# A recurrent-memory attention layer on one core: attention output, output projection and value rows moved one stage later

## The chip, the core and the metric

The kernel runs on one core of a Trainium2 chip. The metric is device time in microseconds of one execution. The core has five engines with instruction streams of their own: TensorE (PE in the profile, with PEld for its weight loads), VectorE (DVE), ScalarE (ACT), GpSimd (POOL) and SyncE (SP). SP computes nothing here and issues DMA transfers; ACT computes and can issue transfers too.

## The reference

Four layers follow each other: A, B, A, B. Layer B is a linear attention and isn't touched. Layer A cuts 2048 tokens into 64 segments of 32. Each segment is attended together with 8 memory rows, and the output of those 8 rows is the memory of the next segment, so segments run strictly one after the other.

```python
for s in range(n_seg):                       # 64 segments
    xs = x[:, s * seg_len:(s + 1) * seg_len, :]
    h = jnp.concatenate([mem, xs], axis=1)   # 8 + 32 rows, 640 wide
    q = jnp.einsum('btd,dhe->bhte', h, Wq)   # 32 heads of 192
    k = jnp.einsum('btd,dhe->bhte', h, Wk)
    v = jnp.einsum('btd,dhe->bhte', h, Wv)
    scores = jnp.einsum('bhqe,bhke->bhqk', q, k) * scale
    scores = jnp.where(mask[None, None], scores, -1000000000.0)
    p = _softmax(scores, axis=-1)
    o = jnp.einsum('bhqk,bhke->bhqe', p, v)
    o = jnp.einsum('bhte,hed->btd', o, Wo)
    mem = o[:, :M, :]
    outs.append(o[:, M:, :])
```

## The kernel before

A layer A has three parts. `A_pre` computes, for all segments at once, keys, queries and values of those 8 rows of each segment that don't depend on the memory, and stores them in DRAM (`kqb_d`, `vb_d`). `A_chain` runs the recurrence. `A_post` makes the attention output of those 8 rows, from what the chain stored in `otb_d`.

`A_chain` is a loop over 64 segments (`s`), each of four rounds (`r`) of 8 heads. Its order is written out by hand (`tc.manual_schedule()`): every engine runs its instructions in the order of the source. A round of the kernel before does this:

- Q projection (`keys_or_queries`, `project`, L443): 20 matmuls in 5 blocks of 4 that run side by side in four column groups of the array.
- From round 1 on, `attend` of the round before (L495), then `extra_v` (L434), two small transfers that bring 8 stored value rows for this round into the tile `V`.
- `to_rows` for Q (L455, L460 to L463): ACT copies PSUM to SBUF, DVE transposes into `QT`. Then `store_o` (L508), which copies the attention output to `OT`.
- K projection, `to_rows` for K (L457, into `KT`), then `wo_round` of the round before (L513): 48 matmuls of `OT` with the resident output weights, accumulated in `W`.
- `scores` (L477 mask, L484 keys by queries), exponential into `E` (L548), `extra_kq` on POOL for the next round (L426 to L430).
- V projection. After three of its five blocks stands the matmul with a block of ones that sums `E` (L557). Then Ln and Exp of the sums on ACT (L563, L564), the multiplication of `E` on DVE (L566), and `v_rows` (L469 on DVE, L471 on ACT), which copies the 32 value rows of four head pairs from PSUM into `V`, DVE and ACT in turn.

After round 3 the segment ends serially: `attend`, `extra_v` for the next segment, `hx_transpose` (L414, new token rows), `store_o` on ACT and DVE (L506), `wo_round`, transpose of `W` (L581), memory rows into `hT` (L582), and only then the next Q projection. With odd segments, `ob` goes out by four transfers (L586).

Part of the projection weights is not kept in SBUF. A table `STREAM` says how many of the five blocks of each of the twelve matrices per segment are loaded anew: two for most, one for V of round 1, none for K of round 0. They land in a ring of three tiles (`wring`, `DEPTH = 3`, L308). `refill` issues the load for the use three places on, after the projection that reads the tile. In the kernel before all loads of the chain, large and small, are issued by SP in source order. Most tiles (`V`, `E`, `OT`, `QT`, `KT`, `hT`) are single-buffered.

Of the kernel before, what the change touches and what calls it, by code (L numbers as in the profile page):

```python
# [100 lines left out]
class Kernel:  # L101
# [180 lines left out]
    def layer_A(self, xn_dram, at_dram, li):  # L282
# [6 lines left out]
        self.vb_d = dram.tile([NSEG, NR, 2, 8, 768], BF16, name=f"vb{li}")  # L289
# [35 lines left out]

    def A_pre(self, xn_dram, li, load, pieces):
# [4 lines left out]
        with tc.tile_pool(name=f"A{li}_pre", bufs=1) as pp, \  # L331
# [15 lines left out]
            vt = pp.tile([P, 2, 768], BF16, name="vst")  # L347
            for r in range(NR):
# [19 lines left out]
                for tb in range(NT):  # L368
                    for g in range(4):
                        ps = ps_.tile([P, 512], F32, name="ps_pre", tag="bank")  # L370
                        for b in range(KC):
                            nc.tensor.matmul(ps[:, 0:384], lhsT=xBTf[:, b, P * tb:P * tb + P],
                                             rhs=wv[b][:, 384 * g:384 * g + 384], start=(b == 0), stop=(b == KC - 1))
                        ev.copy(out=vt[:, g // 2, 384 * (g % 2):384 * (g % 2) + 384], in_=ps[:, 0:384])
                    for t2 in range(TP):
                        nc.scalar.dma_start(out=self.vb_d[:, r, :, TP * tb + t2, :], in_=vt[NSEG * t2:NSEG * t2 + NSEG, :, :])

    def A_chain(self, xn_dram, at_dram, li, load, pieces, wo):
# [4 lines left out]
        with tc.tile_pool(name=f"A{li}_ch", bufs=1) as sp, \  # L383
# [5 lines left out]
            V = sp.tile([P, 768], BF16, name="Vp")  # L389
# [18 lines left out]
            def load_rows(s):  # L408
                for g in range(4):
                    nc.sync.dma_start(out=Hx[32 * g + 8:32 * g + 32, :, :], in_=xv[0:24, s:s + 2, 160 * g:160 * g + 160])  # L410

            def hx_transpose(s):
                hT = sp.tile([P, KC, 32], BF16, name="hT", tag="hT")
                nc.vector.transpose(out=hT[:, :, :], in_=Hx[:, s % 2, :].rearrange("p (j b) -> p b j", b=KC))  # L414
                if s % 2 == 1 and s + 1 < NSEG:
                    load_rows(s + 1)
                return hT

            def load_kqb(s):
                kqb = sp.tile([P, NR, 192], BF16, name="kqb", tag="kqb")  # L420
                nc.sync.dma_start(out=kqb[:], in_=self.kqb_d[s])
# [10 lines left out]
            def extra_v(s, r):  # L432
                for G in range(2):
                    nc.sync.dma_start(out=V[64 * G + 32:64 * G + 40, :], in_=self.vb_d[s, r, G])  # L434
# [18 lines left out]
            def to_rows(ps, m):  # L453
# [4 lines left out]
                else:  # L458
                    rv = raw[:, :].rearrange("p (g i j) -> p g i j", i=3, j=32)
                    nc.vector.transpose(out=qv[:, :, 0, 8:40], in_=rv[:, :, 0, :])  # L460
                    nc.vector.transpose(out=qv[:, :, 3, 8:40], in_=rv[:, :, 2, :])
# [3 lines left out]
            def v_rows(ps, g, eng):  # L465
                o = V[64 * (g // 2):64 * (g // 2) + 32, 384 * (g % 2):384 * (g % 2) + 384]
                i = ps[32 * g:32 * g + 32, 0:384]
# [21 lines left out]
            def attend(E):  # L489
                O = pop.tile([P, 2, 512], F32, name="ps_o", tag="o")  # L490
                for x in range(2):
                    for v0, mm, e, i, row in ((0, 128, 0, 0, 0), (256, 128, 1, 2, 0), (128, 64, 0, 1, 0), (192, 64, 1, 1, 64)):
                        for G in range(2):
                            o0 = 120 * x + 40 * i
                            nc.tensor.matmul(O[row:row + mm, G, o0:o0 + 40],  # L495
                                             lhsT=V[64 * G:64 * G + 40, 384 * x + v0:384 * x + v0 + mm],
                                             rhs=E[64 * G:64 * G + 40, 80 * x + 40 * e:80 * x + 40 * e + 40],
                                             start=(x == 0 and v0 == 0), stop=(x == 1 and v0 == 192),
                                             tile_position=(64 * G, row), skip_group_check=True)
# [10 lines left out]
            def wo_round(W, r, OT):  # L510
                for c in range(12):
# [4 lines left out]

            for g in range(4):
                nc.sync.dma_start(out=Hx[32 * g:32 * g + 8, 0, :], in_=self.A_mem0[:, 160 * g:160 * g + 160])
# [6 lines left out]
            hT = hx_transpose(0)  # L525
            for s in range(NSEG):
                if s % 2 == 0:
                    ob = sp.tile([P, 2, 160], BF16, name="ob", tag="ob")
                otb = sp.tile([P, NR, 12, 8], BF16, name="otb", tag="otb")
                W = pop.tile([P, 512], F32, name="ps_w", tag="w")  # L530
                E = None
                for r in range(NR):
                    pq = keys_or_queries(hT, "Q", r)
                    if E is not None:
                        O, OT = attend(E)
                        extra_v(s, r)
                    to_rows(pq, "Q")
                    if E is not None:
                        store_o(O, OT, 0, "s")
                        store_o(O, OT, 1, "s")  # L540
                        nc.gpsimd.tensor_copy(out=otb[:, r - 1, :, :], in_=OT[:, :, 0:8])  # L541
                    pk = keys_or_queries(hT, "K", r)
                    to_rows(pk, "K")
                    if E is not None:
                        wo_round(W, r - 1, OT)
                    S = scores()
                    E = sp.tile([P, 160], BF16, name="E", tag="E")
                    nc.scalar.activation(out=E[:], in_=S[:, 0:160], func=ACT.Exp, scale=scale)  # L548
                    if r + 1 < NR:
                        extra_kq(kqb, r + 1)  # L550
                    elif s + 1 < NSEG:
                        kqb = load_kqb(s + 1)
                        extra_kq(kqb, 0)
                    pv = pqp.tile([P, 512], F32, name="ps_qkv", tag="qkv")
                    w = weights("V", r)
                    project(hT, pv, w, "V", range(KC - 2))
                    nc.tensor.matmul(S[:, 256:416], lhsT=self.ones_blk[:, :], rhs=E[:, :], start=True, stop=True,  # L557
                                     skip_group_check=True)
                    project(hT, pv, w, "V", range(KC - 2, KC))
                    if STREAM["V", r]:  # L560
                        refill()
                    rc = sp.tile([P, 160], F32, name="rc", tag="rc")
# [256 lines left out]
```

The softmax here doesn't subtract the row's maximum and nothing guards it: scores larger than these inputs give would overflow.

## Time and profile before

| what | value |
|---|---|
| median of 3 runs | 5683.79 us (5674.05 to 5689.94) |
| profiled execution, own time | 5693.49 us |
| its span, first to last instruction | 5690.9 us |
| mean granted TensorE clock | 0.881 |
| TensorE matmul, busy | 73% |
| VectorE, busy | 41% |
| ScalarE, busy | 37% |
| HBM traffic over the span | 229 GB/s |

The page's slices show the two layers A as two long stretches of about 275 GB/s, and layers B between and behind them with little traffic. The busy shares are means over both kinds of layer, so a question about the chain is put to windows inside it. In the timeline a row gives start and length in us, engine, line, what is written from what is read, and in brackets how long the engine stood idle before it and what ended that. In the chain of waits each row is a piece of the path, followed back from the end. Matmul lengths overlap since they are pipelined: the issue time of a group is read from start to start.

### The profile page before, as it was taken

The numbers are of one execution on the slowest core, as the hardware profiler recorded it, in microseconds if no ns is written. First come the engines' busy times: TensorE is split into PE (matmuls) and PEld (weight loads), VectorE is DVE, ScalarE is ACT, GpSimd is POOL, SyncE is SP. The second block draws the span as 40 slices with busy tenths as digits, with TensorE's granted clock in tenths as the row PEclk, the third lists the DMA queues.
The fourth block names the chain that finished last, engine by engine and source line by source line (L and its number), as shares of the span: only waits on it lengthen the run. The fifth ranks groups of instructions, "written<-read, shape, count | busy, mean of one in ns | idle before, by whom it ended". The sixth has DMA issues, their size and how long they took to land.

```text
span 5690.9 us, 186473 instructions
## 1 busy us (share of the span) xinstructions
PE 4165.3 (73%) x79816; PEld 2489.4 (44%) x79816; DVE 2323.7 (41%) x6110; ACT 2122.3 (37%) x5373; POOL 631.5 (11%) x3095
## 2 busy tenths in 40 slices
PE   3877777777777777727858777777777777777568
PEld 2744444444444444413337444444444444444333
DVE  2234344434444444238432344444344434442483
ACT  1234444444444444213112344444444444443230
POOL 0011111111111111000000111111111111110000
PEclk9989888889998889859979898898899888999789
DMA  8777777777777878540077787777787877885301
GB/s 269 184 268 274 278 270 280 273 268 279 275 278 273 282 269 283 164 131 1 22 217 192 249 279 273 279 274 275 269 292 273 279 269 272 282 284 178 117 23 34
DMA packets 537065, 1312.99 MB, mean 231 GB/s; under 512 B 215376, under 2 KB 339248, under 8 KB 536240
## 3 DMA queue, kind: packets, MB, share of 16 engines
q1 hardware_dynamic: 361648, 1223.99, 61.7%
q10 hardware_dynamic: 174592, 77.09, 5.5%
q8 instruction: 629, 10.31, 0.7%
q14 instruction: 196, 1.61, 0.1%
HBM read 1213.43 MB, written 87.46 MB: 229 GB/s over the span
## 4 chain that ended last, share of the span: by engine, by line
PE 47%; DMA 23%; DVE 18%; ACT 7%; issue 3%; ACTq 1%; SPq 0%; DVEq 0%; POOL 0%; POOLq 0%
PE ps_qkv L443 20%; DMA wring<-wstK 9%; DVE Vp L469 7%; PE ps_o L495 6%; PE ps_w L513 5%; DMA wring<-wstQ 4%; DVE KT L457 3%; ACT raw L455 3%; PE ps_pre L358 3%; ACT Vp L471 3%; PE ps_s L484 2%; PE ps_num L627 2%; PE ps_bqk L627 2%; PE ps_kv L627 2%; DMA Vp<-vb 2%
## 5 line engine op out<-in xcount | busy, mean ns | idle before, releaser
L443 PEld LDWEIGHTS <-hT 128*32 128x32 bf16 x30720 | 739.3, 103 | 799.0 <-issue 410.0
L469 DVE CAST Vp<-ps_qkv 32x384 bf16<-32x384 f32 x1024 | 563.6, 550 | 1121.7 <-PE ps_qkv L443 960.1
L443 PE MATMUL ps_qkv<-wring,hT 128*32 128x384 bf16 x10752 | 749.2, 353 | 146.7 <-DMA wring<-wstQ 97.5
L495 PE MATMUL ps_o<-E,Vp 40*128 40x40 bf16 (+1 forms) x8192 | 507.7, 197 | 423.0 <-DVE Vp L469 253.2
L455 ACT ACTIVATE raw<-ps_qkv 128x384 bf16<-128x384 f32 x1024 | 501.9, 490 | 520.8 <-PE ps_qkv L443 498.9
L471 ACT ACTIVATE Vp<-ps_qkv 32x384 bf16<-32x384 f32 x1024 | 493.3, 482 | 519.4 <-DVE Vp L469 519.4
L513 PE MATMUL ps_w<-wo_res,OT 128*32 128x160 bf16 x24576 | 618.8, 259 | 72.8 <-ACT OT L508 71.8
L495 PEld LDWEIGHTS <-Vp 40*128 40x128 bf16 (+1 forms) x8192 | 319.3, 100 | 749.4 <-DVE Vp L469 315.6
L513 PEld LDWEIGHTS <-OT 128*32 128x32 bf16 x24576 | 539.0, 108 | 134.2 <-ACT OT L508 86.0
L443 PE MATMUL ps_qkv<-wQ,hT 128*32 128x384 bf16 x6144 | 407.1, 377 | 117.0 <-DVE hT L582 85.5
L460 DVE STREAM_TRANSPOSE QT<-raw 128x128 bf16<-128x128 bf16 x512 | 159.4, 311 | 726.2 <-ACT raw L455 726.2
L443 PE MATMUL ps_qkv<-wK,hT 128*32 128x384 bf16 x7168 | 455.4, 377 | 0.0
L443 PE MATMUL ps_qkv<-wV,hT 128*32 128x384 bf16 x6656 | 403.9, 340 | 2.7 <-issue 2.7
L457 DVE STREAM_TRANSPOSE KT<-raw 128x384 bf16<-128x384 bf16 x512 | 295.9, 578 | 250.1 <-ACT raw L455 248.2
L548 ACT ACTIVATE E<-ps_s 128x160 bf16<-128x160 f32 x512 | 155.2, 303 | 610.3 <-PE ps_s L484 610.3
L484 PE MATMUL ps_s<-QT,KT 128*40 128x40 bf16 (+1 forms) x6144 | 183.9, 190 | 239.4 <-DVE KT L457 239.1
L508 ACT ACTIVATE OT<-ps_o 128x240 bf16<-128x240 f32 x896 | 290.1, 368 | 101.5 <-PE ps_o L495 85.0
L426 POOL COPY QT<-kqb 128x32 bf16<-128x32 bf16 x512 | 106.7, 208 | 1975.3 <-PE ps_s L484 1032.3
L484 PEld LDWEIGHTS <-KT 128*40 128x40 bf16 x6144 | 140.8, 100 | 299.4 <-issue 298.4
L541 POOL COPY otb<-OT 128x96 bf16<-128x96 bf16 x384 | 100.7, 262 | 1405.6 <-ACT OT L508 1405.6
L563 ACT ACTIVATE rc<-ps_s 128x160 f32<-128x160 f32 x512 | 155.4, 304 | 263.4 <-PE ps_s L557 263.4
L358 PE MATMUL ps_pre<-xBT,wring 128*128 128x128 bf16 x1344 | 184.4, 221 | 4.4 <-DMA wring<-in_A_Wq_dram 3.2
(388 smaller groups left out, 4828.9 us busy)
## 6 DMA issues: line engine op xcount, KB each, us to landing
wring<-wstQ SPq DMA_DIRECT2D x516, 768.0 KB
wring<-wstV SPq DMA_DIRECT2D x387, 768.0 KB
wring<-wstK SPq DMA_DIRECT2D x387, 768.0 KB
wring<-wstV SPq DMA_DIRECT2D x129, 384.0 KB
kqb<-kqb SPq DMA_DIRECT2D x128, 192.0 KB
Vp<-vb SPq DMA_DIRECT2D x1024, 12.0 KB
wo_res<-in_A_Wo_dram SPq DMA_DIRECT2D x8, 1920.0 KB
kqb<-stk ACTq DMA_DIRECT2D x32, 384.0 KB
```

The source lines that it names most:

```text
L358: nc.tensor.matmul(ps[:, P * i:P * i + P], lhsT=w[b][:, P * c:P * c + P], rhs=xBT[:, b, :, 16 * tb:16 * tb + 16], start=(b == 0), stop=(b ...
L443: nc.tensor.matmul(ps[32 * g:32 * g + 32, 0:384], lhsT=hT[:, b, :], rhs=rhs, start=(b == 0), stop=(b == KC - 1), tile_position=(0, 32 * g) ...
L455: nc.scalar.activation(out=raw[:], in_=ps[:, 0:384], func=ACT.Copy)
L457: nc.vector.transpose(out=KT[:, :, 0:32], in_=raw[:, :].rearrange("p (c j) -> p c j", j=32))
L460: nc.vector.transpose(out=qv[:, :, 0, 8:40], in_=rv[:, :, 0, :])
L469: nc.vector.tensor_copy(out=o, in_=i)
L471: nc.scalar.activation(out=o, in_=i, func=ACT.Copy)
L484: nc.tensor.matmul(S[64 * G:64 * G + 40, c0:c0 + q1 - q0], lhsT=KT[:, 3 * g + i, :], rhs=QT[:, g, q0:q1], start=False, stop=False, tile_po ...
L495: nc.tensor.matmul(O[row:row + mm, G, o0:o0 + 40], lhsT=V[64 * G:64 * G + 40, 384 * x + v0:384 * x + v0 + mm], rhs=E[64 * G:64 * G + 40, 8 ...
L508: nc.scalar.activation(out=o, in_=i, func=ACT.Copy)
L513: nc.tensor.matmul(W[32 * g:32 * g + 32, 0:160], lhsT=OT[:, c, 8:40], rhs=wo[:, 12 * r + c, 160 * g:160 * g + 160], start=(r == 0 and c == 0),
L627: nc.tensor.matmul(ps[rows, n0:n0 + nn], lhsT=lhsT_fn(k), rhs=rhs_fn(k, n0, nn), **kw)
```

## The change

The rounds of `A_chain` are put in another order. In round r the order on TensorE is now: Q projection, K projection, attention of round r-1, V projection, scores, five of twelve steps of the output projection of round r-1, the sums of `E`, the other seven steps. The sums of round 0 stand after two blocks of round 1's Q projection. Normalisation (`normalise`) stands behind the output projection, and the value rows are copied around the exponential of the scores. The serial end of a segment keeps its steps, but `hx_transpose` moves ahead into round 3, with `hT` in two buffers.

`V` becomes 1024 columns wide: each head's 192 columns get 64 columns of zeros beside them (`two_heads`), and all attention matmuls have 128 output rows and one tile position per half. `vb_d` and `A_pre` follow this.

All small transfers of the chain (`load_rows`, `load_kqb`, `extra_v`, the stores of `otb` and of `ob`) move from SP's queue to ACT's; `kqb` of the next segment is loaded in round 2; the stores of `otb` and `ob` are issued in round 0 of the next segment. Two query transposes become one instruction, and the second half of `store_o` goes to DVE in all rounds.

```diff
-        self.vb_d = dram.tile([NSEG, NR, 2, 8, 768], BF16, name=f"vb{li}")
+        self.vb_d = dram.tile([NSEG, NR, 2, 8, 1024], BF16, name=f"vb{li}")
...
+    def two_heads(self, ap):
+        d = [list(x) for x in ap.ap]
+        return ap3(ap, [d[0], [320, 2], [1, 192]])
...
-            vt = pp.tile([P, 2, 768], BF16, name="vst")
+            vt = pp.tile([P, 4, 512], BF16, name="vst")
+            nc.vector.memset(vt[:], 0.0)
...
-            V = sp.tile([P, 768], BF16, name="Vp")
+            V = sp.tile([P, 1024], BF16, name="Vp")
...
-                    nc.sync.dma_start(out=Hx[32 * g + 8:32 * g + 32, :, :], in_=xv[0:24, s:s + 2, 160 * g:160 * g + 160])
+                    nc.scalar.dma_start(out=Hx[32 * g + 8:32 * g + 32, :, :], in_=xv[0:24, s:s + 2, 160 * g:160 * g + 160])
...
-                nc.sync.dma_start(out=kqb[:], in_=self.kqb_d[s])
+                nc.scalar.dma_start(out=kqb[:], in_=self.kqb_d[s])
...
-                    nc.sync.dma_start(out=V[64 * G + 32:64 * G + 40, :], in_=self.vb_d[s, r, G])
+                    nc.scalar.dma_start(out=V[64 * G + 32:64 * G + 40, :], in_=self.vb_d[s, r, G])
...
-                    nc.vector.transpose(out=qv[:, :, 0, 8:40], in_=rv[:, :, 0, :])
-                    nc.vector.transpose(out=qv[:, :, 3, 8:40], in_=rv[:, :, 2, :])
+                    nc.vector.transpose(out=qv[:, :, 0:4:3, 8:40], in_=rv[:, :, 0:3:2, :])
...
-                o = V[64 * (g // 2):64 * (g // 2) + 32, 384 * (g % 2):384 * (g % 2) + 384]
-                i = ps[32 * g:32 * g + 32, 0:384]
+                o = self.two_heads(V[64 * (g // 2):64 * (g // 2) + 32, 512 * (g % 2):512 * (g % 2) + 512])
+                i = ps[32 * g:32 * g + 32, 0:384].rearrange("p (e f) -> p e f", e=2)
...
-                    for v0, mm, e, i, row in ((0, 128, 0, 0, 0), (256, 128, 1, 2, 0), (128, 64, 0, 1, 0), (192, 64, 1, 1, 64)):
+                    for k, e, i in ((0, 0, 0), (3, 1, 2), (1, 0, 1), (2, 1, 1)):
                         for G in range(2):
                             o0 = 120 * x + 40 * i
-                            nc.tensor.matmul(O[row:row + mm, G, o0:o0 + 40],
-                                             lhsT=V[64 * G:64 * G + 40, 384 * x + v0:384 * x + v0 + mm],
+                            nc.tensor.matmul(O[:, G, o0:o0 + 40],
+                                             lhsT=V[64 * G:64 * G + 40, 512 * x + 128 * k:512 * x + 128 * k + 128],
                                              rhs=E[64 * G:64 * G + 40, 80 * x + 40 * e:80 * x + 40 * e + 40],
...
-                                             tile_position=(64 * G, row), skip_group_check=True)
+                                             tile_position=(64 * G, 0), skip_group_check=True)
```

The body of a round after the change, with `sums` and `normalise` as the new names of the matmul of L557 and of what was L562 to L566:

```python
pq = pqp.tile([P, 512], F32, name="ps_qkv", tag="qkv")
w = weights("Q", r)
project(hT, pq, w, "Q", range(2))
if r == 1:
    sums(S, E)
    normalise(S, E)
project(hT, pq, w, "Q", range(2, KC))
...
to_rows(pq, "Q")
pk = keys_or_queries(hT, "K", r)
to_rows(pk, "K")
if r == 0 and s > 0:
    nc.scalar.dma_start(out=self.otb_d[s - 1], in_=otb[:, :, :, :].rearrange("p r c t -> p (r c t)"))
    if s % 2 == 0:
        store_rows(s - 2, ob_old)
if r > 0:
    O, OT = attend(E)
    store_o(O, OT, 0, "s")
    extra_v(s, r)
    store_o(O, OT, 1, "v")
...
pv = pqp.tile([P, 512], F32, name="ps_qkv", tag="qkv")
project(hT, pv, weights("V", r), "V", range(KC))
if STREAM["V", r]:
    refill()
S = scores()
v_rows(pv, 0, "v")
v_rows(pv, 1, "s")
E = sp.tile([P, 160], BF16, name="E", tag="E")
nc.scalar.activation(out=E[:], in_=S[:, 0:160], func=ACT.Exp, scale=scale)
v_rows(pv, 2, "v")
v_rows(pv, 3, "s")
if r + 1 < NR:
    extra_kq(kqb, r + 1)
    if r + 2 == NR and s + 1 < NSEG:
        kqb = load_kqb(s + 1)
elif s + 1 < NSEG:
    extra_kq(kqb, 0)
    hT = hx_transpose(s + 1)
    if s % 2 == 0 and s + 2 < NSEG:
        load_rows(s + 2)
if r > 0:
    wo_round(W, r - 1, OT, range(5))
    sums(S, E)
    wo_round(W, r - 1, OT, range(5, 12))
    normalise(S, E)
```

## The prediction, made before the changed kernel ran

> **What bounds the kernel now.** I read the page's slices and DMA queues first, then the windows of one stretch, then the chain of waits over one segment boundary, then TensorE's timeline over one round. The memory update of L582 starts at 331.2 and 2311.0 us in the first A layer (63 times, 62 periods) and at 3195.3 and 5162.0 in the second: (1979.8 + 1966.7) / 124 = 31.83 us a segment, and 128 segments are 4074 of the 5690.9 us. Only they are changed in substance.
>
> Chain of waits, start, length, what:
> ```profile
> 1501.02 6.65 DMA wring<-wstV
> 1507.67 0.04 issue
> 1507.71 0.53 PE ps_qkv L443 x8
> 1508.24 0.02 issue
> 1508.27 0.56 DVE Vp L469
> 1508.82 0.02 issue
> 1508.85 0.49 ACT Vp L471
> ...
> 1511.50 1.36 PE ps_w L513 x48
> 1512.86 0.02 issue
> 1512.88 0.36 DVE wt L581
> 1513.24 0.02 issue
> 1513.26 0.24 DVE hT L582
> 1513.51 0.04 issue
> 1513.55 1.82 PE ps_qkv L443 x20
> ```
> Two things alternate: a weight load 6.65 us from issue to landing, and a serial tail. From the last V matmul (1508.24) to the next segment's first Q matmul (1513.55) is 5.31 us. The value rows are drained by DVE and ACT in turn, never together.
>
> TensorE timeline of a round without a load wait:
> ```profile
> 1517.70 0.35 PE L484 MATMUL ps_s<-QT,KT 128*40 128x40 bf16 x12 [1.21 <-DVE KT L457]
> ...
> 1521.02 0.87 PE L495 MATMUL ps_o<-E,Vp 40*128 40x40 bf16 x15 [0.68 <-DVE Vp L469]
> 1521.82 0.67 PE L443 MATMUL ps_qkv<-wK,hT 128*32 128x384 bf16 x12
> 1522.32 0.50 PE L443 MATMUL ps_qkv<-wring,hT 128*32 128x384 bf16 x8
> 1522.64 1.00 PE L513 MATMUL ps_w<-wo_res,OT 128*32 128x160 bf16 x48
> 1523.58 0.26 PE L477 MATMUL ps_s<-mask_st,ident 128*64 128x160 bf16 x2
> 1524.12 0.35 PE L484 MATMUL ps_s<-QT,KT 128*40 128x40 bf16 x12 [0.28 <-DVE KT L457]
> ```
> Scores to scores is 6.42 us. Starts give the issue times: a projection 0.82 (1521.82 to 1522.64), Wo 0.94, attention 0.80, scores 0.27. Twice a round TensorE stands: for value rows, and for transposed keys.
>
> Windows: two of rounds, one of the boundary; the last three columns are granted clock, DMA share, GB/s:
> ```profile
> 1519.00:1526.00 7.00, 5.93 (x162) 3.69 (x157) 3.17 (x9) 4.02 (x11) 1.38 (x7) 1.00 0.99 359
> 1528.00:1537.00 9.00, 7.61 (x194) 4.94 (x198) 3.97 (x13) 5.05 (x13) 1.50 (x7) 0.94 0.98 366
> 1513.00:1518.00 5.00, 3.24 (x58) 1.70 (x61) 2.04 (x7) 1.28 (x3) 0.60 (x3) 0.75 0.20 56
> ```
> In the rounds the DMA engines are full; at the boundary they are nearly empty, because the ring of three weight tiles is full, and no projection frees one. So a faster TensorE meets the loads.
>
> **What the Trainium skill says.** "TensorEngine Tiling (Array Packing)", Key Properties: a change of tiling mode drains TensorE. The trace agrees: 16 attention matmuls that alternate 64- and 128-column tiles take 0.80 us, 12 score matmuls of like size in one mode 0.27. "DMA: Bandwidth & Descriptors", Issuing engines are not separate DMA queues: another issuing engine saves only issue time, since the same 16 engines move the bytes. The trace has that time, 0.28 to 0.37 us of SP for each small transfer; no run shows yet what ACT pays for these. "TensorE: Matmul & The Clock Gate", HAM oscillation: idle gaps lower the array's clock. The trace agrees: the first 20 matmuls of a segment take 1.82 us against 0.96 later, and the boundary window has clock 0.75.
>
> **The change, part by part.** A round is now Q, K, attention of r-1, V, scores, 5/12 of Wo, softmax sums, 7/12 of Wo. From the diff and the durations above:
>
> *Waits that go.* Attention had waited for value rows and E (568.9 + 347.8 us over 512 rounds by the row of L495) and, for 68.4 us, for the vb transfer; now Q and K projections lie between (1.6 us). The normalisation (Ln 0.30, Exp 0.34, multiply 0.30) is hidden there too. Scores had waited 239.1 us for KT; raw copy 0.50 and transpose 0.58 now hide behind attention and V.
>
> *What is late next.* E. ACT has its first value copy ahead of E and waits for DVE's: after V's end 0.57 + 0.50 + 0.33 = 1.4 us to E, while TensorE has only scores 0.45 and five Wo steps 0.35. It stands about 0.6 us before the sums. Round: three projections 2.45 + attention 0.55 + 1.4 + sums and lag 0.4 + the rest of Wo 0.5 = 5.3 us, against 6.42.
>
> *Padded values.* Same matmul count; three mode changes go per attention. Bounds 0.36 (16 at the scores' rate) and 0.80; I take 0.55 with lag.
>
> *ACT transfers.* Fourteen issues per segment move to ACT (8 vb, 1 kqb, 1 otb, Hx and attn 2 each on average). At SP's 0.28 to 0.37 that is 4.6 us; ACT is busy 14.1 us of 31.8 (0.44), so no bound in sum. Upper price 0.62, as for vb<-vst on ACT. Queued behind: after the vb pair the value copy, already later because of DVE (no cost at 0.3); behind four attn stores E of round 0 (0.8 us every second segment, partly hidden by K1's load; I count nothing, 0.4 on average at most); behind four Hx loads Ln of round 3, on the tail: 4 x 0.36 = 1.4 us every second segment, 0.65 on average with overlap. The fourth Hx load also waits for the semaphore of the next Q0 load, which lands before by my times below. SP is freed: there four attn stores held the next weight load from 1514.09 to 1517.11.
>
> *Tail now.* V end to next Q: DVE 0.56, ACT 0.49, DVE 0.57, ACT 0.50 (2.16), Ln, Exp, multiply 1.0 with hand-overs (3.2), attention to 3.75, OT copy to 4.2, Wo 1.36 to 5.6, transpose and cast to 6.25. Against 5.31 it is 0.9 longer, because the normalisation now follows the value copies; with Hx 6.9.
>
> *Before the chain.* vb rows grow from 1536 to 2048 bytes. TensorE's waits on vb<-vst and what follows are some 65 us; a third would be 22, nothing the lower end. I take 6. Merged query transposes (0.31 to 0.58, I take 0.45) and the early hT transpose are off the path.
>
> **The loads.** A segment moves ten loads of 768 KB and one of half, 8.26 MB, and 0.54 MB of small things (0.57 after). At the 355 GB/s mean of full windows (359, 366, and 346 in another of 14 us) a load with its share of the small ones is 0.838 MB, 2.36 us. By the packet records of that boundary a load into an empty queue starts 1.0 us after issue, and TensorE goes on 1.1 to 2.0 us after its last packet; I take 1.4. A load issues when the projection three uses before it ends. From Q0's start (Q0 1.8 at low clock): projections end Q0 1.8, K0 2.7, V0 3.5, Q1 5.9. Then, landing and end: K1 6.6, 6.9; V1 7.75, 8.3; Q2 10.7, 11.4; K2 13.0, 13.35; V2 15.4, 15.75; Q3 17.75, 18.9; K3 20.1, 20.45; V3 22.45, 22.8. From K2 on the load, not TensorE, ends last at every step but Q3. With the tail the period is 29.7 us. It saves 2.1 us a segment: 128 x 2.1 = 270, less 6, from the profiled execution's own 5693.49 us (span 5690.9) gives about 5425. The shown median is 10 below it, so **5415 us**.
>
> The same reckoning for the kernel before gives about 30.5 where 31.83 was measured. It is short on scatter among loads, which is why the rivals below vary that term.
>
> **Rivals.** *The loads come slower still.* Packet records of loads that follow each other closely average 2.48 us; 7.5 loads lie between Q0 and V3, so 0.9 more: 30.7, a gain of 1.15 x 128 = 147, about 5540. For it: the shortfall just named. Against: small transfers no longer hold weight loads back on SP. Chance 0.25.
>
> *The clock stays up and loads run at the bare 2.21 us (0.786 MB at 355).* Q0 then takes 0.9 less, 7.5 x 0.15 = 1.1 less to V3, Wo in the tail 0.5 less: 27.2, 4.6 x 128 = 590, about 5095. For it: the tail has TensorE work in its first 2 us. Against: three idle stretches remain. Chance 0.20.
>
> *ACT becomes the bound, slower than before.* In-order ACT pays 0.62 per issue and waits for DMA semaphores: Hx +1.1 and the burst of otb and attn about +2.0 in every second segment, vb +0.26 in three rounds: 1.55 + 0.8 = 2.3 a segment, if the loads cover none. It decides from 2.1 us a segment; with the Hx loads' semaphore wait 0.4 more, 128 x 0.6 = 75: about 5750. For it: 0.62 stands in the trace for ACT. Against: that row is a 64-partition store, and a small store on ACT (attn<-obB) has 0.31. Chance 0.12.
>
> The order listing shows the moves as the diff has them, so that the change does nothing is no case.
>
> **How the numbers follow.** Forecast 0.43, own range 5330 to 5490 (period 29.0 to 30.3). Slower loads 0.25, better overlap 0.20, ACT 0.12. The whole range runs from 5100, which takes in most of the good case, to 5640, past the slow-load case at 2.6 us a load. No change that can be told means within 0.3%, 17 us: 0.03 lies there, from the slow-load case. Faster 0.85, slower 0.12.
>
> **What would show it.** Attention's idle time on value rows and E nearly gone; sums waiting for E at about 0.6 us a round; load waits of TensorE up from 146.7 us (the ps_qkv<-wring row) to some 500 (0.2 + 1.1 + 1.0 + 0.7 + 0.95 a segment above); the chain inside segments mostly weight loads; GB/s in the chain near 295 instead of 275; tails of 6.3 and 7.6 us in turn. Wrong would be: ACT stretches where its transfers sit between Exp and the value copies and TensorE waits for ACT; a load share under 0.85 with TensorE still waiting; or rounds above 6.4 us.

## The result, and the profile after

The changed kernel takes 5721.14 us (median of 4 runs, 5716.01 to 5736.02), the kernel before 5686.86 us beside it: a ratio of 1.0067, 95% interval 1.004 to 1.0094. It is a little slower, where 5415 us and a gain were forecast; the time lies above the whole range. The kernel before itself had medians from 5684 to 5724 us on different chips, so kernels are compared by their ratios to a kernel before that ran beside them, not by their times. The profiled execution took 5722.32 us, its span is 5720.5 us, and the mean granted clock fell from 0.881 to 0.870.

Since a segment keeps its steps, I cut the trace of each kernel at the same points and took means over the 124 boundaries: Q0 is the moment when the memory rows stand in `hT` (some 0.05 us before a segment's first Q matmul), V3 the start of the first value copy of round 3, and the tail runs from V3 to the next Q0. The period is the time from one Q0 to the next. These figures come from one profiled execution of each kernel; the four executions of one kernel lie up to 46 us apart (`norm_first`), which is 0.4 us a segment.

| us a segment | before | after | predicted after |
|---|---|---|---|
| Q0 to V3 | 26.43 | 24.22 | 22.8 |
| tail, V3 to next Q0 | 5.40 | 7.81 | 6.9 |
| of it, V3 to multiply done | 0.78 | 4.05 | 3.2, and 0.65 for Hx |
| to first and last attention matmul | 1.10, 2.43 | 4.32, 4.79 | 3.75 (last) |
| to start of Wo and to DVE's transpose behind it | 3.21, 4.83 | 5.50, 7.24 | 4.2, 5.6 |
| period | 31.83 | 32.03 | 29.7 |

So the rounds did gain 2.2 us and the tail gave back 2.4. In every second segment, nearly all of which load token rows (Hx), the tail is 8.23 us, in the others 7.39; 7.6 and 6.3 were predicted.

From the costliest groups of the page of the kernel after (line, engine, operation, tiles, count; busy and mean ns of one; idle time before it, and what ended most of that):

```profile
L452 PE MATMUL ps_qkv<-wring,hT 128*32 128x384 bf16 x10752 | 748.0, 353 | 367.3 <-DMA wring<-wstK 178.0
...
L503 PE MATMUL ps_o<-E,Vp 40*128 40x40 bf16 x8192 | 210.0, 181 | 301.6 <-DVE E L533 201.8
...
L526 PE MATMUL ps_s<-E,ones_blk 128*128 128x160 bf16 x512 | 120.7, 236 | 348.0 <-ACT E L582 348.0
...
L531 ACT ACTIVATE rc<-ps_s 128x160 f32<-128x160 f32 x512 | 155.3, 303 | 119.0 <-DMA Hx<-xn 101.8
```

The waits for streamed weights grew from 146.7 to 367.3 us, short of the 500 expected. The sums wait 348.0 us for `E`, 0.68 us a round, as predicted (0.6). The last row is ACT's: 101.8 us in which Ln stood behind the issues of the Hx loads.

The chain of waits of the kernel after, over one boundary and the round behind it (start, length, what), and the start of Ln in the tail that follows:

```profile
1508.77 0.27 ACTq L443
1509.04 0.06 ACT OT L516
1509.09 0.04 issue
1509.13 6.12 DMA Vp<-vb
1515.25 0.05 issue
1515.29 0.46 PE ps_o L503 x15
...
1516.26 1.82 PE ps_w L521 x47
...
1518.72 3.18 PE ps_qkv L452 x40
...
1522.83 0.38 ACTq L426
...
1545.97 0.38 ACTq L417
1546.36 0.04 issue
1546.40 0.38 ACTq L417
1546.78 0.04 issue
1546.82 0.38 ACTq L417
1547.20 0.05 issue
1547.25 0.31 ACT rc L531
```

Four things are to be seen. The attention of round 3 waits for the stored value rows (`Vp<-vb`, two transfers of 16 KB), which were under way for 6.12 us. `Wo` takes 1.82 us where the kernel before took 1.36 in the chain shown with the prediction (means: 1.74 and 1.62). The first 40 matmuls of the next segment take 3.18 us. And ACT, in order, issues `ob` stores (L426) and Hx loads (L417) on the path.

TensorE's timeline of the kernel after, over two rounds (start, length, line, tiles; in brackets the idle time before):

```profile
1530.19 0.23 PE L526 MATMUL ps_s<-E,ones_blk 128*128 128x160 bf16 x1 [0.83 <-ACT E L582]
...
1533.33 0.51 PE L452 MATMUL ps_qkv<-wring,hT 128*32 128x384 bf16 x8 [1.01 <-DMA wring<-wstK]
1533.77 0.37 PE L503 MATMUL ps_o<-E,Vp 40*128 40x40 bf16 x16
1534.07 0.67 PE L452 MATMUL ps_qkv<-wV,hT 128*32 128x384 bf16 x12
1535.60 0.51 PE L452 MATMUL ps_qkv<-wring,hT 128*32 128x384 bf16 x8 [0.87 <-DMA wring<-wstV]
...
1537.60 0.23 PE L526 MATMUL ps_s<-E,ones_blk 128*128 128x160 bf16 x1 [0.67 <-ACT E L582]
```

Inside the rounds the plan works: this attention starts with no wait at all (means of rounds 0 to 2: 0.17, 0.10 and 0.02 us, before 0.77, 0.64 and 0.25), and takes 0.30 us from start to start (1533.77 to 1534.07) instead of 0.80. What it waited for before has become two waits for weights, 1.01 and 0.87 us, in a round of 7.41 us.

### The profile page after: what moved, and what is told of

The parts are those of the page before. It is cut to its first block, busy times and chain, and to the rows that moved or that the text cites. A ratio compares the mean times of both kernels' runs of the same rounds, so it can differ in the third digit from the quotient of the medians.

```text
span 5720.5 us, 185022 instructions
## 1 busy us (share of the span) xinstructions
PE 3916.7 (68%) x79816; PEld 2351.5 (41%) x79816; DVE 2474.0 (43%) x5984; ACT 1969.5 (34%) x4989; POOL 630.8 (11%) x3095
## 4 chain that ended last, share of the span: by engine, by line
DMA 42%; PE 32%; DVE 11%; ACT 8%; ACTq 3%; issue 3%; SPq 1%; DVEq 0%; POOL 0%
DMA wring<-wstV 18%; PE ps_qkv L452 12%; DMA wring<-wstK 10%; DMA Vp<-vb 6%; PE ps_w L521 4%; ACT Vp L479 3%; PE ps_pre L364 3%; DVE Vp L477 3%; PE ps_num L653 2%; DMA vb<-vst 2%; PE ps_bqk L653 2%; PE ps_kv L653 2%; PE ps_o L503 2%; PE pp L630 2%; ACTq L417 1%
## 5 line engine op out<-in xcount | busy, mean ns | idle before, releaser
L452 PEld LDWEIGHTS <-hT 128*32 128x32 bf16 x30720 | 802.5, 104 | 1200.0 <-issue 823.6
L452 PE MATMUL ps_qkv<-wring,hT 128*32 128x384 bf16 x10752 | 748.0, 353 | 367.3 <-DMA wring<-wstK 178.0
L477 DVE CAST Vp<-ps_qkv 32x384 bf16<-32x384 f32 x1024 | 558.1, 545 | 496.5 <-ACT Vp L479 320.2
L521 PE MATMUL ps_w<-wo_res,OT 128*32 128x160 bf16 x24576 | 718.2, 267 | 67.8 <-ACT OT L516 66.8
L521 PEld LDWEIGHTS <-OT 128*32 128x32 bf16 x24576 | 509.4, 110 | 411.2 <-issue 310.0
L533 DVE TENSOR_TENSOR E<-E,rc 128x160 bf16<-128x160 bf16 x512 | 166.6, 325 | 693.6 <-ACT rc L532 693.6
L469 DVE STREAM_TRANSPOSE QT<-raw 128x256 bf16<-128x256 bf16 x512 | 228.0, 445 | 460.6 <-ACT raw L464 453.6
L503 PE MATMUL ps_o<-E,Vp 40*128 40x40 bf16 x8192 | 210.0, 181 | 301.6 <-DVE E L533 201.8
L526 PE MATMUL ps_s<-E,ones_blk 128*128 128x160 bf16 x512 | 120.7, 236 | 348.0 <-ACT E L582 348.0
L503 PEld LDWEIGHTS <-Vp 40*128 40x128 bf16 x8192 | 166.1, 95 | 453.7 <-issue 282.7
L514 DVE CAST OT<-ps_o 128x240 bf16<-128x240 f32 x512 | 208.9, 408 | 204.8 <-ACT OT L516 193.2
L516 ACT ACTIVATE OT<-ps_o 128x240 bf16<-128x240 f32 x512 | 188.3, 368 | 198.2 <-PE ps_o L503 192.0
L531 ACT ACTIVATE rc<-ps_s 128x160 f32<-128x160 f32 x512 | 155.3, 303 | 119.0 <-DMA Hx<-xn 101.8
```

The source lines that it names most:

```text
L452: nc.tensor.matmul(ps[32 * g:32 * g + 32, 0:384], lhsT=hT[:, b, :], rhs=rhs, start=(b == 0), stop=(b == KC - 1), tile_position=(0, 32 * g) ...
L469: nc.vector.transpose(out=qv[:, :, 0:4:3, 8:40], in_=rv[:, :, 0:3:2, :])
L477: nc.vector.tensor_copy(out=o, in_=i)
L503: nc.tensor.matmul(O[:, G, o0:o0 + 40], lhsT=V[64 * G:64 * G + 40, 512 * x + 128 * k:512 * x + 128 * k + 128], rhs=E[64 * G:64 * G + 40, 8 ...
L514: nc.vector.tensor_copy(out=o, in_=i)
L516: nc.scalar.activation(out=o, in_=i, func=ACT.Copy)
```

## The experiments

The theory after this reading: the loads take a part of what the rounds gain, and the tail takes the rest, through (a) Hx issues on ACT, (b) value rows that land last, (c) the normalisation behind the value copies, (d) a low clock. Rival: the loads alone set the period, so that whatever the tail gains is waited for again in the rounds. Ratios are to the kernel before, run beside each.

**1 and 2: which queue.** `hx_on_sp` is the kernel after with one issue back on SP, `small_on_sp` with all of the chain's small transfers there.

```diff
-                    nc.scalar.dma_start(out=Hx[32 * g + 8:32 * g + 32, :, :], in_=xv[0:24, s:s + 2, 160 * g:160 * g + 160])
+                    nc.sync.dma_start(out=Hx[32 * g + 8:32 * g + 32, :, :], in_=xv[0:24, s:s + 2, 160 * g:160 * g + 160])
```

> The changed kernel with its token-row loads (Hx) issued by SP instead of ACT. Theory 'the tail gives it back': these loads stand before Ln on ACT in every second segment's tail, where V to memory update is 8.23 us against 7.39 in the others, and Ln comes 1.66 us later. 62 such tails shorten by some 1.4 to 1.7 us: about 5620 us, ratio to before 0.985 to 0.99. Theory 'weight loads set the pace': what the tail saves comes back as load waits; 5700 to 5720, ratio 1.00 to 1.006.

> The changed kernel with all small transfers of the chain back on SP's queue; order of rounds and padding as changed. Theory 'the tail gives it back': as hx_on_sp, plus or minus little, 5600 to 5640. Theory 'the ACT queue's transfers land late' (the vb rows took 6 us from issue in one tail): still 0.3 to 0.5 us a segment better than hx_on_sp, 5560 to 5600. Theory 'SP holds the weight loads back again': slower than hx_on_sp by 0.5 to 1 us a segment, 5680 to 5740.

`hx_on_sp`: 5642.78 us, ratio 0.9875 (0.9823 to 0.9927). The multiplication ends 3.22 us after V3 in all segments, the tail is 7.40, the period 31.61. One edit turns a change that is 0.7% slower into one that is 1.2% faster. How much a segment gains is known only roughly: 0.42 us by the two traces, 0.9 us by the two ratios; the profiled execution of `hx_on_sp` was the slowest of its four, 5667.66 us. `small_on_sp`: 5745.26 us, 1.0044 (1.0026 to 1.0062), tail 8.28. That is near the 5680 to 5740 expected if SP held the weight loads back, but not for that reason: Q0 to V3 is 23.92 us, shorter than the 24.21 of `hx_on_sp`, and only the tail is longer. TensorE's waits for the value rows, first of `hx_on_sp`, then of `small_on_sp` (us in total, times, longest):

```profile
PE ps_o L503 <- DMA Vp<-vb: 188.1, 182, 3.0
```

```profile
PE ps_o L503 <- DMA Vp<-vb: 316.1, 125, 4.3
```

With Hx gone from the tail, the wait for these rows is twice as long as in the kernel after (86.1 us): they had been hidden under the Hx issues. On SP, where their issue also stands in order with the weight loads, they come later still. By the packet records (a packet is one piece that a DMA engine moves) the time from issue to the last packet is 4.03 us (median) in the kernel after and 4.25 in `small_on_sp`: ACT's queue is hardly a faster way in. What counts is what else is moving: in the kernel after the two transfers for round 0, issued in the tail when the DMA engines have little to do, are in after 1.33 and 1.37 us, the two for round 3 after 4.13 and 4.81 (medians).

**3 and 4: the loads.** Both kernels, with only the first of two streamed blocks loaded and used for both. The second block of those projections is left out of what is computed.

```diff
+                if short:
+                    nc.sync.dma_start(out=t[:, 0:1, :], in_=self.wst[m, r][:, 0:1, :])
...
-                return [res[m, r, b] for b in range(KC - ns)] + [t[:, i, :] for i in range(ns)]
+                return [res[m, r, b] for b in range(KC - ns)] + [t[:, 0 if short else i, :] for i in range(ns)]
```

> The kernel before, with only the first of the two streamed blocks of each weight loaded in the chain and used for both (the second block of the projection is left out of the loads, so the weights computed with differ); instructions on TensorE are the same. Theory 'weight loads set the pace': load waits go, period near 6.42 x 3 + 10.8 = 30.1 us, about 5460. Theory 'order alone': the same 5690.

> The changed kernel with the same halving of the streamed weights. Theory 'weight loads set the pace': its waits of TensorE for loads (367 us) go and rounds fall to the shortest seen, 5.2, 5.5, 5.5 and 10.7 us: period near 27, about 5100 to 5200, clearly under the halved kernel before (ratio of the two 0.93 to 0.95). Theory 'the tail and the ACT queue alone': it keeps its place, some 0.5% above the halved kernel before.

Before: 5546.35 us, 0.9715 (0.9674 to 0.9757), period 30.73. After: 5262.72 us, 0.9216 (0.9177 to 0.9256), period 28.45. Both are slower than expected (about 5460, and 5100 to 5200), but their ratio, 0.949, is as expected. The full loads cost the kernel before 1.10 us a segment and the kernel after 3.58, of which 3.16 lie between Q0 and V3; the other 0.42 are in the tail, where the small transfers land earlier too. With half the bytes the new order is worth 30.73 - 28.45 = 2.28 us; with all of them, -0.20. A round of the kernel before is 6.42 us between two exponentials, one of the kernel after 5.58 (medians), where 5.3 was predicted. TensorE of `half_loads_after` over one such round:

```profile
1506.17 0.35 PE L494 MATMUL ps_s<-QT,KT 128*40 128x40 bf16 x12 [0.29 <-DVE KT L468]
1506.45 0.53 PE L523 MATMUL ps_w<-wo_res,OT 128*32 128x160 bf16 x20
1507.81 0.23 PE L528 MATMUL ps_s<-E,ones_blk 128*128 128x160 bf16 x1 [0.83 <-ACT E L584]
...
1510.19 0.37 PE L505 MATMUL ps_o<-E,Vp 40*128 40x40 bf16 x16
...
1511.98 0.35 PE L494 MATMUL ps_s<-QT,KT 128*40 128x40 bf16 x12 [0.30 <-issue]
```

No wait for a load is left; `KT` (0.29) and `E` (0.83) hold the round. The prediction had the second (0.6), but not the first. The tail tells more: where no Hx load stands in it, it is 6.36 us, with attention right behind the multiplication (3.27 against 3.21). The prediction had 6.25 for just this tail. So the tail's own steps were sized well, and what came on top of them came from transfers.

**5: the padding alone**, on the kernel before.

```diff
-                                             lhsT=V[64 * G:64 * G + 40, 384 * x + v0:384 * x + v0 + mm],
+                                             lhsT=V[64 * G:64 * G + 40, 512 * x + 128 * k:512 * x + 128 * k + 128],
```

> The kernel before with the zero-padded value blocks alone (order of rounds and queues as before). Attention there is on the path in every round; padding takes three mode changes from it, 0.80 to some 0.45 us. Theory 'weight loads set the pace': a small part stays, 5640 to 5690, ratio 0.993 to 1.0. Theory 'TensorE's chain sets the pace': 512 x 0.35 = 180 us, about 5510, ratio 0.968.

5714.32 us, 0.9993 (0.9973 to 1.0012): no change, as expected if the loads set the pace. TensorE's timeline of `padding_alone`:

```profile
1520.84 0.27 PE L501 MATMUL ps_o<-E,Vp 40*128 40x40 bf16 x8 [0.68 <-DVE Vp L475]
1521.35 0.26 PE L501 MATMUL ps_o<-E,Vp 40*128 40x40 bf16 x7 [0.25 <-ACT Vp L477]
```

The matmuls are shorter, but in the old order they wait for value copies between them, so most of the time saved becomes idle time. The kernel before has that second wait too, hidden in the row of 15 matmuls in the prediction: by start times (medians) the tenth matmul comes 0.51 us after the second in both kernels, and the K projection behind attention 0.80 us after it before and 0.71 here. The change of tile size shows in the same start times: where the tile goes from 128 to 64 columns or back, the next matmul comes 0.11 to 0.14 us later in the kernel before, and 0.00 us later at the same places here.

**6: the normalisation.** `hx_on_sp` with Ln, Exp and multiplication of round 3 ahead of the last value copy and `hx_transpose` behind it.

```diff
-                    v_rows(pv, 3, "s")
+                    if r + 1 < NR:
+                        v_rows(pv, 3, "s")
...
                     normalise(S, E)
+                    if r + 1 == NR:
+                        v_rows(pv, 3, "s")
```

> hx_on_sp with Ln, Exp and the multiplication of round 3 ahead of the last value copy on ACT, and hx_transpose behind them. Theory 'the normalisation behind the value copies makes the tail long': multiply ends 0.9 us earlier than 3.22 after V, 128 x 0.8 = 100 us less than hx_on_sp, ratio 0.970. Theory 'the vb rows of round 3 land last': attention there already waits until 3.76 and its last matmul until 4.47 though E is ready at 3.22, so nearly nothing is gained, ratio 0.985 to 0.988.

5642.93 us, 0.9869 (0.9831 to 0.9906), the same as `hx_on_sp`. The multiplication ends 2.75 us after V3 instead of 3.22, and the last attention matmul starts at 4.41 instead of 4.47: the end that counted was another, the value rows.

**7 and 8: the value rows.** `vb_early` is `hx_on_sp` with the attention in round 3 ahead of the K projection, and with it the issue of that round's stored value rows. Since it also moves TensorE's work, `round3_rows_left_out` moves nothing: it is `hx_on_sp` without these two transfers in round 3.

```diff
+                        if r + 1 < NR:
+                            extra_v(s, r)
```

> hx_on_sp with attention ahead of the K projection in round 3, so that the vb rows of that round are asked for one projection and one load wait earlier. Theory 'the vb rows land last in the tail': last attention matmul 4.47 to 3.5 after V, 0.8 x 128 = 100 us less, ratio 0.970. Theory 'normalisation': no gain, 0.985 to 0.99.

> hx_on_sp, with the two transfers that bring the eight stored value rows of round 3 left out (V keeps those of round 2, so this part of the computation is not done); order and instruction counts are otherwise the same. Theory 'the tail's attention waits for these rows, which land last behind the weight loads': attention starts right after the multiplication (3.3 us after the first value copy of round 3 instead of 3.76 to 4.47) and the tail falls from 7.40 to 6.2 to 6.4 us; 126 segments x 1.1 = 139 us, some 5500 us, ratio 0.960 to 0.968, as in vb_early. Rival 'vb_early gained because the K projection behind the attention fills TensorE before the load of V': here nothing moves, the tail stays above 7.2 us and the ratio stays at hx_on_sp's 0.9875.

`vb_early`: 5519.31 us, 0.9637 (0.9605 to 0.9668), tail 6.26, period 30.49. `round3_rows_left_out`: 5534.2 us, 0.9715 (0.9686 to 0.9745), tail 6.35, period 30.54; its ratio lies a little over the 0.960 to 0.968 expected. In both the attention starts at 3.27 us, right behind the multiplication. The tail's chain of `round3_rows_left_out`:

```profile
1526.45 0.34 DVE E L533
1526.79 0.04 issue
1526.83 0.39 PE ps_o L503 x16
...
1527.72 1.07 PE ps_w L521 x48
```

Where 6.12 us of `Vp<-vb` stood, E leads into attention, and the multiplication ends at 3.22 us as before, so it is not ACT's time for two issues that was saved. So these rows cost 1.05 us a segment by the traces (7.40 - 6.35; by the ratios 0.7 in this kernel and 1.1 in `vb_early`), and starting their transfer one projection and its load wait earlier is enough to take the cost away. The rival falls for this term: the rounds, 24.2 us in all three kernels, took nothing back.

**9: the clock.** `hx_on_sp` with 28 matmuls whose result nobody reads, 20 ahead of the attention of round 3, 4 ahead of Wo and 4 behind it.

```diff
+            def keep_busy(S, n):
+                for _ in range(n):
+                    nc.tensor.matmul(S[:, 416:512], lhsT=self.ones_blk[:, :], rhs=self.mk[:, 0:96], start=True, stop=True,
+                                     skip_group_check=True)
```

> hx_on_sp with 28 matmuls of 96 columns, whose result nobody reads, in the tail's idle stretches of TensorE (20 before attention, 4 behind it, 4 behind Wo). Theory 'low clock in the tail and in Q0': Wo of the tail goes from 1.65 to some 0.95 us and Q0 with K0 from 3.2 to some 1.8; at least the tail's 0.7 us a segment shows, 90 us, up to 180 with Q0 and K0: ratio 0.956 to 0.972. Theory 'it costs or does nothing': 0.985 to 1.0.

5538.72 us, 0.9677 (0.965 to 0.9705), period 30.67. Windows of 4 us on either side of a boundary, first of `hx_on_sp`, then of `array_kept_busy` (window, length, busy time of PE, PEld, DVE, ACT, POOL with counts, then granted clock, DMA share, GB/s):

```profile
1506.25:1510.25 4.00, 2.33 (x64) 1.82 (x64) 0.94 (x3) 0.55 (x2) 0.26 (x1) 0.65 0.50 200
1510.25:1514.25 4.00, 3.94 (x52) 2.05 (x56) 0.94 (x4) 1.10 (x3) 0.00 (x0) 0.50 0.22 71
```

```profile
1515.46:1519.46 4.00, 2.96 (x89) 2.23 (x89) 1.08 (x4) 0.55 (x2) 0.26 (x1) 1.00 0.58 222
1519.46:1523.46 4.00, 3.46 (x82) 2.00 (x82) 1.95 (x6) 1.10 (x3) 0.29 (x2) 1.00 0.42 138
```

In the second row of each, the new segment gets through 52 and 82 matmuls in the same 4 us, at clock 0.50 and 1.00. The tail falls to 7.09 us and Q0 to V3 to 23.58: 0.94 us a segment for work that does nothing. Q0 and K0 together fall from 2.89 to 1.82 us, as expected; Wo of the tail falls to 1.23 us, not to the 0.95 expected.

**10: all of it.** `hx_on_sp` with the edits of `norm_first`, `vb_early` and 14 + 4 + 4 unread matmuls.

> hx_on_sp with norm_first, vb_early and 14 + 4 + 4 unread matmuls that keep TensorE busy in the tail. If the tail's terms are in series (theory), they add once the value rows land in time: multiplication at 2.75 us instead of 3.2, attention right behind it, Wo and Q0 at the higher clock: tail 5.2 to 5.5 us, Q0 to first value copy of round 3 about 23.6, period 28.7 to 29.2 us: 5290 to 5370 us, ratio 0.925 to 0.94. Rival 'the loads take back what the tail gains' (the ring is full at the boundary, so an earlier Q0 only waits longer for the same loads): period not under 30.2 us, 5480 to 5520 us, ratio 0.96 or more.

5410.47 us, 0.9508 (0.9475 to 0.9541), period 29.51, tail 5.90: faster than both kernels. It misses the 0.925 to 0.94 and the tail of 5.2 to 5.5 us expected. The chain of its tail shows what I had left out, the unread matmuls themselves (L537), which stand between Wo and attention:

```profile
1509.51 0.60 PE ps_w L521 x28
1510.11 0.70 PE ps_s L537 x14
1510.81 0.32 PE ps_o L503 x16
```

So attention starts at 3.05 us where the multiplication was done at 2.73; with these 0.32 us taken off, the tail would still be 5.58 us, and the rest of the miss was not traced. With 29.51 the rival's 30.2 is refuted: what the tail gains stays gained.

**11 and 12: the stores of `otb` and `ob`**, from `all_together`: moved on ACT behind the exponential and value copies of round 0, or to SP behind V0's load.

```diff
-                    if r == 0 and s > 0:
-                        nc.scalar.dma_start(out=self.otb_d[s - 1], in_=otb[:, :, :, :].rearrange("p r c t -> p (r c t)"))
...
                     v_rows(pv, 3, "s")
+                    if r == 0 and s > 0:
+                        nc.scalar.dma_start(out=self.otb_d[s - 1], in_=otb[:, :, :, :].rearrange("p r c t -> p (r c t)"))
```

> all_together with the stores of otb and ob moved on ACT's queue from ahead of the attention of round 0 to behind the exponential and value copies of that round. Theory 'the burst of stores holds E of round 0 back, with the rounds and all their loads behind it': in segments with the four ob stores the stretch from Q0 to the first value copy of round 3 was about 0.35 to 0.7 us longer; it becomes equal in both kinds, the mean falls from 23.62 to about 23.4 us or less, 126 x 0.2 to 0.35 = 25 to 45 us, ratio 0.943 to 0.947. Rival 'the load of K1 and V1 hides it': ratio stays at 0.951, the second load issue of a segment (V0) comes earlier, the later ones don't.

> all_together with the stores of otb and ob taken off ACT: SP issues them behind the load that V of round 0 frees. Theory 'five stores in a row occupy ACT for 2.1 us, and whatever ACT does next in round 0 or 1 waits': with ACT free, segments with the four ob stores reach the first value copy of round 3 as early as the others (23.3 to 23.45 instead of 23.79 us), mean 23.35 to 23.45 instead of 23.62, a gain of 126 x 0.2 = 25 us: ratio 0.944 to 0.948. Rival 'on SP the 2.1 us hold back the next weight load (that of Q in round 1) just as long': that load is issued when Q1 ends, about 2.8 us after V0's; if the stores are not done by then, the later loads of these segments come up to 0.5 us later and the ratio is 0.951 or more.

`stores_behind_E`: 5518.58 us, 0.9651 (0.9626 to 0.9676), where 0.943 to 0.947 was expected: worse than `all_together`. Timeline of one segment with the five stores:

```profile
1520.22 0.35 ACTq L592 DMA_DIRECT2D otb<-otb  x1
...
1520.67 1.64 ACTq L426 DMA_DIRECT2D attn<-ob  x4
...
1522.36 0.30 ACT L531 ACTIVATE rc<-ps_s 128x160 f32<-128x160 f32 x1 [1.71 <-DMA otb<-otb]
...
1523.44 0.37 PE L503 MATMUL ps_o<-E,Vp 40*128 40x40 bf16 x16 [1.87 <-DVE E L533]
```

The burst holds ACT from 1520.22 to 1522.31, and Ln stands behind it: TensorE waits 1.87 us. In these segments Q0 to V3 is 25.84 us, in the others 23.31. So the burst did hold `E` of round 0 back (in segments with the stores it comes 0.60 us later than in the others in `all_together`, 0.21 here), but its new place is worse than its old one. `stores_on_sp`: 5464.36 us, 0.9571 (0.9543 to 0.96), where 0.944 to 0.948 was expected. It is also worse than `all_together`, though only by 0.6%, and the two intervals all but touch. `E` of round 0 now starts 4.51 and 4.49 us after Q0, in segments without and with the stores, so ACT is freed as expected. But SP issues the load behind K1 at 8.13 us instead of 6.57 in the segments with stores; the trace names the `otb` store as what SP waited for (104.1 us in 52 cases). V3 is also 0.37 us later than in `all_together` in segments without stores; that was not traced to a cause.

## Why the prediction was wrong

The period was to be 29.7 us and was 32.03; 126 x 2.33 = 294 us, and 5415 + 294 = 5709 is close to the 5721 measured, so these segments account for the miss. It has two parts, 0.91 in the tail and 1.42 ahead of V3.

**The tail.** The step that failed is "Waits that go": the prediction took the 68.4 us that attention had waited for vb as a wait that goes, and never asked when the rows of the last round would land in the new order. They cost 1.05 us a segment (shown by experiments 7 and 8). The prediction had quoted that the same 16 engines move the bytes, and applied it to the price of issuing and not to the time of landing. The Hx issues were costed at 1.4 us every second segment, 0.65 on average; ACT's Ln comes 1.66 us later in these segments (3.85 against 2.19), and with the rows late anyway they cost 0.41 (7.81 - 7.40). The rest of the tail, 6.35 us with both gone, is near the 6.25 predicted. So the 0.91 is 1.05 for the rows, 0.24 less for Hx and 0.10 for the rest. Wo was taken from one row at 1.36, where its mean had been 1.62; it took 1.74 in the kernel after and takes 1.49 to 1.59 where the rows are not awaited.

**Ahead of V3.** By the issue times of the loads, which follow the end of a projection, in us after Q0:

| | V0 | Q1 | V1 | Q2 | V2 | Q3 | V3 |
|---|---|---|---|---|---|---|---|
| predicted | 3.5 | 5.9 | 8.3 | 11.4 | 15.75 | 18.9 | 22.8 |
| kernel after | 3.97 | 6.80 | 9.17 | 12.93 | 17.07 | 20.42 | 24.19 |
| array_kept_busy | 2.94 | 5.89 | 8.34 | 12.09 | 16.53 | 20.04 | 23.51 |

From Q2 to V3 the kernel after needs 11.26 us where 11.4 was predicted: the pace of the loads was right, and the rival of slower loads is not what happened. What failed is the start: 0.90 us by Q1, and 0.66 more from V1 to Q2 (3.76 instead of 3.1). The loads did not do this: with half their bytes Q1 and Q2 end at nearly the same times, 6.93 and 12.94 us. Three terms were mis-sized.

- The clock. A low clock was counted for Q0 alone, but K0 and V0 have it too: they take 2.12 us from the end of Q0 (the load issue at 1.85) where 1.7 was taken, and 1.71 with the clock kept up. "TensorE: Matmul & The Clock Gate", HAM oscillation, in the Trainium skill, names idle gaps as the cause of a lower clock, and the runs agree; the prediction had put a higher clock into a rival only.
- The stores ahead of `E` of round 0, "I count nothing". They make Q1 0.70 us later in every second segment (7.15 against 6.45), of which 0.51 is left at V3: 0.25 on average. In `small_on_sp`, where SP issues them, Q1 ends equally early in both kinds of segment (within 0.05 us).
- `E` of round 1, from V1 to Q2. It was to be done 1.4 us after the end of the V projection, with DVE's first value copy starting at once. That copy starts 0.60 us late (mean) and `E` is done at 1.98 us. DVE, in order, has other work first, as the timeline shows: the last V matmuls, then `KT`, then the second half of the copy to `OT`, which the change moves to DVE (L514), then the value copy (L477), ACT's copy behind it, and `E`.

```profile
1527.79 0.34 PE L452 MATMUL ps_qkv<-wring,hT 128*32 128x384 bf16 x4
1527.82 0.58 DVE L466 STREAM_TRANSPOSE KT<-raw 128x384 bf16<-128x384 bf16 x1
...
1528.43 0.41 DVE L514 CAST OT<-ps_o 128x240 bf16<-128x240 f32 x1
...
1528.76 0.54 DVE L477 CAST Vp<-ps_qkv 32x384 bf16<-32x384 f32 x1
...
1529.33 0.48 ACT L479 ACTIVATE Vp<-ps_qkv 32x384 bf16<-32x384 f32 x1 [1.73 <-DVE Vp L477]
...
1529.83 0.30 ACT L582 ACTIVATE E<-ps_s 128x160 bf16<-128x160 f32 x1
```

In rounds 2 and 3, where TensorE waits for loads, the same copy starts 0.05 and 0.08 us after V's end. With half the loads it is late in all three rounds (0.61, 0.42 and 0.39 us), which is why a round without load limit is 5.58 and not 5.3 us. This is read from the traces; no run gives DVE less to do there.

**What was right.** Attention hardly waits inside the rounds; its 16 matmuls cost 0.30 and not 0.80 us, below the 0.55 taken. The drain at a change of tiling mode that the Trainium skill's "TensorEngine Tiling (Array Packing)", Key Properties, names is gone, and the 0.30 is near the rate of the scores in one mode; but a part of the 0.80 was the wait for the last value copy, which the prediction read as tiling too (experiment 5). Its 568.9 + 347.8 us of waits also add those of weight loads and matmuls, which pass at the same time: the page has 423.0 us of idle time before the attention matmuls. The sums wait 0.68 us; the loads become the bound from K2 on, as predicted (Q2 to V3 takes 11.26 us, with half the loads 7.78). `A_pre` and all else outside the segments came to some 4 us, where 6 was taken (5720.5 - 126 x 32.03 against 5690.9 - 126 x 31.83). The rival "ACT becomes the bound" had the sign, and named Hx and the burst; but its price per issue (0.62) was not seen, the issues in a burst are 0.41 to 0.45 us apart, and the largest single part of the loss, the rows in flight, was not its mechanism. That its 5750 us is near the 5721 measured is luck.

The warning stood in the prediction itself: the same reckoning gave 30.5 for the kernel before, 1.3 too short, and the difference was put down to scatter among loads. That was not looked into. A sum that misses the known kernel by 1.3 us can hardly carry a gain of 2.1.

## What to carry to other kernels

When a small transfer shares the DMA engines with a saturated stream, cost the time from issue to landing under that load, not its size: here 16 KB took 1.3 us beside idle DMA engines and up to 4.8 us (medians) beside the weight loads, and the last of them stood on the serial tail. Before putting issues on a computing engine's queue, look at which of its instructions follow them in order: four issues put off the next activation by 1.66 us here, and there may be no better place for them in the order. Ask also what a computing engine still has to do when the work you count on reaches it: DVE's first value copy started 0.60 us late. A reordering that fills a stretch that loads bound loses part of its gain: Q0 to V3 fell by 4.17 us with half the loads and by 2.20 with all. What was taken off the serial tail was kept (1.05 us of tail, 1.07 of period in experiment 8), and so was the gain of unread work that keeps the clock up.

## What the runs showed of the hardware

A queue of its own didn't carry small transfers past large ones: 4.03 us from issue to last packet on ACT's queue against 4.25 on SP's, with full loads, and 2.39 on ACT's with half loads. Most of this passes before the first packet, as the profile counts them, starts: 3.18 of the 4.03 us (medians), against 0.9 us for the transfers issued beside nearly idle engines. "DMA: Bandwidth & Descriptors", Queues, rings and completion order, in the Trainium skill, says that each engine takes turns between the queues that have work and drains a whole packet, typically 9 to 17 descriptors, before it switches. What the profile counts as a packet is smaller: a piece of 6144 bytes for the loads. If each of these is one descriptor, nine of them at the 355 GB/s of 16 engines take 2.5 us: an estimate from that page's figure. The measured wait is of this size; how the pieces are grouped is shown by no run here.

TensorE's clock could be bought: 28 matmuls of 96 columns brought the mean granted clock of the first 2 us of a segment, and of the 2 us ahead of it, from between 0.5 and 0.6 to over 0.9, and 0.94 us a segment with it.

A change between tiles of 64 and 128 columns cost TensorE 0.11 to 0.14 us each time in the attention of the kernel before (medians of 512); zeros that make all tiles 128 wide took this away.
